# Normalising attention probabilities on GpSimd, with another written order of the first stage

## The chip, the cores and the metric

The kernel runs on one core of one Trainium2 chip. A core has five engines that run side by side, each with its own queue of instructions that it takes strictly in order: TensorE (PE in the profile, its weight loads PEld), VectorE (DVE), ScalarE (ACT), GpSimd (POOL) and SyncE (SP), which here only issues DMAs. The metric is device time in microseconds (us) for one execution.

## The reference

Three layers in a row, all in float32. The first is a windowed attention with block summaries:

```
k_sum = k.reshape(B, H, nb, 32, D).max(axis=3);  v_sum = v.reshape(...).mean(axis=3)
scores = concat[ scale*q@k.T where |i-j| < 16 else -1e9,  scale*q@k_sum + log(32) ]
a = exp(scores - max);   a = a / (sum(a) + 1e-9);   x = a @ concat[v, v_sum]
```

with 2 batches, 8 heads, 768 positions and head size 64. Its result, 1536 tokens of width 512, goes through `h = x @ w_in`, a PReLU with a slope for each of 2048 channels, and `@ w_out`. The last layer has four experts, `relu(x @ w1[e]) @ w2[e]`, summed with normalised weights. The attention inputs q and k are eight times as large as their first draw.

## The kernel before

**Precision.** A matmul operand is split into a high part (rounded by ScalarE) and a low part (the difference), and a product is three matmuls: high by high, high by low, low by high.

**First stage.** Attention and the first group of four of the sixteen 128-wide slices of the PReLU layer are done together. Attention is cut into 24 half tiles, numbered 0 to 23: 128 tokens by half of the heads. A 256-token block of the first group needs four half tiles (block 0 needs half tiles 0 to 3). The order of this stage is not left to a scheduler: `ORDER` (line 51) is a list of 695 short words, each one step, and every engine gets its instructions in the order of that list, inside `tc.manual_schedule()` (line 878). A word is a two-letter step and a number; a `g` or `v` behind the number moves the step to GpSimd or VectorE (line 880). The dictionary `stage` (line 864) says what a step is:

- `ka`, `va` load K and V by DMA, `kb`, `vb` reduce them over blocks on VectorE, `kc` copies the block maxima beside the keys; `vc` transposes the block sums on TensorE, `ve` (VectorE) and `vd` (ScalarE) write their two halves as means into the two value buffers.
- `fa`, `fb`, `fc` load keys, queries and values of a half tile.
- `sa` scores (TensorE), `sb` mask and row maximum (VectorE, line 225), `sc` exponential with row sums (ScalarE, line 234), `na` adds 1e-9 (VectorE, line 241), `nb` takes reciprocals (VectorE, line 244), `nc` multiplies the probabilities by them (`a_norm`, line 246), `ta` transposes (TensorE), `tb` copies the transposed block to SBUF (ScalarE), `xa` multiplies with the values (TensorE), `xb` and `xc` write high and low part of x (ScalarE, VectorE line 294).
- `wa` loads a slice ("piece") of `w_in` or `w_out` as raw 64-bit numbers; `wb` to `wj` turn it into float32 high and low parts: seven VectorE steps (`wb wd we wf wg wh wj`) and two on ScalarE (`wc`, `wi`). Pieces 0 to 3 are the first group's `w_in`, 4 to 7 its `w_out`, 8 to 15 the second group's.
- `la` multiplies (12 matmuls of 128x256), `lb` to `le` apply the PReLU and split; `ma` and `mb` are the product with `w_out` and the copy of its sum. `pa` is the first product of the second group.

`a_norm` has three forms:

```
if on != "a":
    eng = nc.vector if on == "v" else nc.gpsimd
    eng.tensor_tensor(pp, pp, r[:, :, None].to_broadcast([P, 4, NK]), op=ALU.mult)
    return
for u in range(4):
    nc.scalar.activation(pp[:, u], pp[:, u], AF.Copy, scale=r[:, u:u + 1])
```

The probability buffer `sm` exists three times, the PSUM buffer shared by `la`, `ta` and `vc` three times, the raw buffer of a piece three times.

**Later stages.** Behind the first stage come the other three groups of the PReLU layer and then the experts; their instructions are ordered by a scheduler when the program is built. GpSimd subtracts low parts there (line 387).

Of the kernel before, what the change touches and what calls it, by code (L numbers as in the profile page):

```python
# [48 lines left out]


ORDER = (
# [34 lines left out]
)  # L86
MASK_OFF = -1.0e9 * math.sqrt(D)
EXP_LOW = float((1023 - 127 + 20) << 20)
# [984 lines left out]
```

## Time and profile before

| what | value |
|---|---|
| time of 3 runs | median 838.79 us, 838.59 to 838.93 |
| the profiled execution | 837.95 us |
| its span, first to last instruction | 836.2 us |
| busy: PE, PEld | 814.4 us (97%), 745.3 us (89%) |
| busy: DVE, ACT, POOL | 618.2 us (74%), 427.4 us (51%), 294.0 us (35%) |
| chain that ended last, by engine | PE 92%, ACT 4%, DVE 2%, DMA 1% |

The profile follows one execution. Matmuls overlap each other, and the ends shown for them are modelled, so that a busy PE is not a PE at its peak. The chain is followed back from the last instruction, at each step to what released it or to the instruction before it on its engine. All but the first 152 us run after the first stage.

### The profile page before, as it was taken

Reading aid. Unit: us, or ns where it says so; the run is one execution under the profiler, and the core shown is the slowest. Engines: PE = TensorE matmul, PEld = TensorE weight load, DVE = VectorE, ACT = ScalarE, POOL = GpSimd, SP = SyncE. Lnnn points to the kernel's source line nnn. Section 1 sums busy time; section 2 is a strip of 40 time slices with the busy share of each in tenths; the row PEclk is TensorE's granted clock in tenths of the full one; section 3 lists DMA queues with packets and bytes.
Section 4 is the critical chain, followed back from the end, with each engine's and each line's share of the span. In section 5 each row is a group of like instructions: output and inputs, shape, how many; then the busy total and the mean of one; then the engine's idle time right before and its main releaser. Section 6 shows DMA issues by size and latency. Waiting matters only on the chain.

```text
span 836.2 us, 14453 instructions
## 1 busy us (share of the span) xinstructions
PE 814.4 (97%) x5000; PEld 745.3 (89%) x5000; DVE 618.2 (74%) x1315; ACT 427.4 (51%) x1050; POOL 294.0 (35%) x265
## 2 busy tenths in 40 slices
PE   3799999999999999999999999999999999999998
PEld 3699999888888888988988988988999999999997
DVE  6998667999994446587687687687667677768765
ACT  4999995543442323454454454455455454455430
POOL 0000000000013100376886886889243444354330
PEclk9799999999999999999999999999999999999999
DMA  9999412233222100266866867879776756767621
GB/s 321 283 299 298 156 46 102 101 100 102 84 92 74 53 1 0 101 223 229 304 234 231 290 215 252 289 240 321 241 228 203 256 197 229 238 217 231 200 74 75
DMA packets 97496, 155.37 MB, mean 186 GB/s; under 512 B 9872, under 2 KB 48272, under 8 KB 97424
## 3 DMA queue, kind: packets, MB, share of 16 engines
q1 hardware_dynamic: 96848, 154.18, 55.0%
q8 instruction: 39, 0.64, 0.3%
q14 instruction: 33, 0.27, 0.1%
q10 hardware_dynamic: 576, 0.28, 0.1%
HBM read 106.71 MB, written 47.71 MB: 185 GB/s over the span
## 4 chain that ended last, share of the span: by engine, by line
PE 92%; ACT 4%; DVE 2%; DMA 1%; issue 0%; ACTq 0%
PE l L536 48%; PE cb L655 16%; PE l2q L777 13%; PE cd L655 8%; PE ca L655 4%; PE s L215 1%; ACT sm L234 1%; ACT sm L253 1%; PE xps L277 1%; PE pt L259 1%; DMA alpha_sb<-in_alpha 1%; ACT ptb L152 1%; DMA kw<-in_kw 1%; DVE vs L179 0%; DVE sm L225 0%; DVE vcat L192 0%
## 5 line engine op out<-in xcount | busy, mean ns | idle before, releaser
L387 POOL TENSOR_TENSOR w0l<-ra,w0h 128x256 fp32r<-128x256 f32 (+1 forms) x32 | 36.8, 1151 | 357.4 <-ACT w0h L386 357.4
L824 DVE SCALAR_TENSOR_TENSOR acc<-l,prob_sb,acc 128x512 f32<-128x512 f32 x101 | 74.5, 745 | 24.7 <-PE l L536 24.6
L788 DVE SCALAR_TENSOR_TENSOR acc<-l2q,prob_sb,acc 128x256 f32<-128x256 f32 x156 | 71.2, 479 | 27.3 <-PE l2q L777 25.4
L536 PE MATMUL l<-xh,w0h 128*128 128x512 f32 (+1 forms) x240 | 84.6, 352 | 0.1
L536 PE MATMUL l<-gh,w1h 128*128 128x512 f32 (+1 forms) x240 | 83.4, 350 | 0.0
L536 PE MATMUL l<-xl,w0h 128*128 128x512 f32 (+1 forms) x240 | 83.3, 347 | 0.0
L536 PE MATMUL l<-xh,w0l 128*128 128x512 f32 (+1 forms) x240 | 83.2, 347 | 0.0
L536 PE MATMUL l<-gh,w1l 128*128 128x512 f32 (+1 forms) x240 | 83.0, 347 | 0.0
L536 PE MATMUL l<-gl,w1h 128*128 128x512 f32 (+1 forms) x240 | 81.5, 347 | 0.0
L536 PE MATMUL l<-w1h,gh 128*128 128x512 f32 x192 | 75.6, 394 | 0.0
L536 PE MATMUL l<-w1h,gl 128*128 128x512 f32 x192 | 75.2, 392 | 0.0
L536 PE MATMUL l<-w1l,gh 128*128 128x512 f32 x192 | 75.1, 391 | 0.0
L678 ACT ACTIVATE u<-cb 128x384 f32<-128x384 f32 x64 | 31.3, 489 | 51.7 <-PE cb L655 51.7
L561 DVE SCALAR_TENSOR_TENSOR l<-m,beta,l 128x512 f32<-128x512 f32 (+1 forms) x60 | 38.6, 646 | 23.8 <-ACT m L555 23.6
L555 ACT ACTIVATE m<-l 128x512 f32<-128x512 f32 (+1 forms) x60 | 30.6, 512 | 46.6 <-PE l L536 46.3
L536 PEld LDWEIGHTS l<-xh,w0h 128*128 128x128 f32 x240 | 45.5, 189 | 6.2 <-ACT ptb L152 0.3
L536 PEld LDWEIGHTS l<-gh,w1h 128*128 128x128 f32 x240 | 45.5, 189 | 5.7
L536 PEld LDWEIGHTS l<-gh,w1l 128*128 128x128 f32 x240 | 45.5, 189 | 5.6
L536 PEld LDWEIGHTS l<-xl,w0h 128*128 128x128 f32 x240 | 45.4, 189 | 5.5
L536 PEld LDWEIGHTS l<-gl,w1h 128*128 128x128 f32 x240 | 45.4, 189 | 5.5
L536 PEld LDWEIGHTS l<-xh,w0l 128*128 128x128 f32 x240 | 45.4, 189 | 5.6
L387 POOL TENSOR_TENSOR w0l<-s,w0h 128x512 fp32r<-128x512 f32 x32 | 47.8, 1513 | 2.9 <-ACT w0h L386 2.9
(165 smaller groups left out, 2527.7 us busy)
## 6 DMA issues: line engine op xcount, KB each, us to landing
raw<-in_wa SPq DMA_DIRECT2D x32, 512.0 KB, 3.8
rb<-in_wb SPq DMA_DIRECT2D x16, 512.0 KB, 4.5
ra<-in_wb SPq DMA_DIRECT2D x32, 256.0 KB, 3.6
dt<-xh SPq DMA_DIRECT2D x28, 256.0 KB, 3.4
dt<-xl SPq DMA_DIRECT2D x28, 256.0 KB, 4.3
bh<-dt SPq DMA_DIRECT2D x28, 256.0 KB, 3.7
bl<-dt SPq DMA_DIRECT2D x28, 256.0 KB, 3.6
q<-in_qh SPq DMA_DIRECT2D x24, 256.0 KB, 5.2
```

What stands on the lines that cost most here:

```text
L152: nc.scalar.activation(dst, src, AF.Copy)
L215: nc.tensor.matmul(sp[:, u], q[:, u // 2, u % 2], kw[:, :, u // 2, u % 2], start=True, stop=True)
L234: nc.scalar.activation(sm[:, u], sm[:, u], AF.Exp, bias=mx[:, u:u + 1], scale=-1.0, accum_out=sume[:, u:u + 1],)
L387: nc.gpsimd.tensor_tensor(lo, src, hi.bitcast(F32), op=ALU.subtract)
L536: ins = nc.tensor.matmul(ps, a, c, start=(i == 0), stop=(i == n - 1))
L555: nc.scalar.activation(m, gs[i, c0][0], AF.Relu, scale=-1.0)
L561: nc.vector.scalar_tensor_tensor(ps, m, beta[:, i:i + 1], ps, op0=ALU.mult, op1=ALU.add)
L655: nc.tensor.matmul(ps, l, r, start=(first and i == 0), stop=(i == len(terms) - 1), skip_group_check=True)
L678: nc.scalar.activation(v[name], ps, AF.Copy)
L777: nc.tensor.matmul(ps, l, r, start=(first and j == 0), stop=(j == len(terms) - 1), skip_group_check=True)
L788: nc.vector.scalar_tensor_tensor(dst, ps, pe, dst, op0=ALU.mult, op1=ALU.add)
L824: nc.vector.scalar_tensor_tensor(acc2[:, t], ps, pe, acc2[:, t], op0=ALU.mult, op1=ALU.add)
```

## The change

Only the text of `ORDER` is another. It holds the same 695 steps. 22 of the 24 `nc` steps (all but half tiles 2 and 16) carry a `g`: there one GpSimd `tensor_tensor` of 128x480 takes the place of four ScalarE activations of 128x120. All other steps stay on their engines, but nearly all stand at another place. What follows the first stage is the same on each engine, instruction by instruction. The table differs in all its lines; of it two:

```diff
@@ -49,40 +49,40 @@
 ORDER = (
-    "wa5 wd5 wb5 we5 ka01 wc5 kb01 ka00 fa2 kb00 kc00 fb2 sa2 wf5 wa3 wg5 fa0 wh5 wb3 wd3 fb0 wi5 ka03 "
...
+    "wa5 wb5 wc5 wa1 wd5 wa0 we5 wf5 ka01 ka00 ka03 wb1 wg5 wd1 fa4 fb2 wh5 wc1 wi5 wf1 wb0 fa2 ka02 "
...
```

On GpSimd the first rows after start-up were, in the kernel before (`w0l`, `s` and `ra` belong to the experts, `vs` to the block sums):

```order
7 L853 MEMSET vs 128x480
8 L387 ISA
9 L387 TENSOR_TENSOR w0l<-ra,w0h 128x256
10 L396 TENSOR_TENSOR s_3682<-ra 128x256
11 L397 TENSOR_TENSOR s_3682<-s_3682,ra 128x256
```

and are now (`sm` is the probabilities, `r` the reciprocals):

```order
7 L853 MEMSET vs 128x480
8 L250 ISA
9 L250 TENSOR_TENSOR sm<-sm,r 128x480 x22
10 L387 TENSOR_TENSOR w0l<-ra,w0h 128x256
11 L396 TENSOR_TENSOR s_3616<-ra 128x256
```

So the 22 multiplications stand ahead of all other work of GpSimd, on an engine that had none in this stage.

On ScalarE, about where the first batch's value means are written (`vcat`, line 190), there stood before (line 253 is the normalising, 234 the exponential, 152 a copy, 318 a step of a piece):

```order
25 L190 ACTIVATE vcat_102<-vsps 24x512
26 L190 ACTIVATE vcat_103<-vsps 24x512
27 L253 ACTIVATE sm<-sm,r 128x120 x4
28 L152 ACTIVATE ptb<-pt 120x512
29 L234 ACTIVATE sm,sume<-sm,mx 128x120 x4
30 L152 ACTIVATE w0h<-t 128x512
```

and now:

```order
21 L190 ACTIVATE vcat_102<-vsps 24x512
22 L190 ACTIVATE vcat_103<-vsps 24x512
23 L234 ACTIVATE sm,sume<-sm,mx 128x120 x4
24 L318 ACTIVATE e<-e,ebias 128x512
25 L152 ACTIVATE xh<-xps 128x2x128
26 L152 ACTIVATE ptb<-pt 120x512
```

The exponential of half tile 7 now stands directly behind the two `vcat` writes.

On VectorE, after its own half of the `vcat` writes (line 192), there stood before:

```order
99 L192 TENSOR_SCALAR vcat_102<-vsps 24x512
100 L192 TENSOR_SCALAR vcat_103<-vsps 24x512
101 L241 TENSOR_SCALAR r<-sume 128x4
102 L338 SCALAR_TENSOR_TENSOR e<-raw,e 128x512
103 L244 RECIPROCAL r<-r 128x4
104 L330 SCALAR_TENSOR_TENSOR t<-raw,t 128x512
```

and now, there and at the reciprocals of half tiles 5 (row 134) and 6 (row 139):

```order
103 L192 TENSOR_SCALAR vcat_102<-vsps 24x512
104 L192 TENSOR_SCALAR vcat_103<-vsps 24x512
105 L323 TENSOR_SCALAR t<-raw 128x512
106 L356 TENSOR_TENSOR w0l<-t,w0h 128x512
107 L241 TENSOR_SCALAR r<-sume 128x4
...
134 L244 RECIPROCAL r<-r 128x4
135 L334 TENSOR_SCALAR e<-e 128x512
136 L330 SCALAR_TENSOR_TENSOR t<-raw,t 128x512
137 L241 TENSOR_SCALAR r<-sume 128x4
138 L338 SCALAR_TENSOR_TENSOR e<-raw,e 128x512
139 L244 RECIPROCAL r<-r 128x4
```

Row 107 reads the row sums of half tile 7; before, row 101 read those of half tile 6, whose exponential stood ahead of the `vcat` writes.

## Rows read from the trace of the kernel before

**Rows 1.** Busy time by stretch; its first line names the columns.

```profile
core 0: us, PE busy (x) PEld busy (x) DVE busy (x) ACT busy (x) POOL busy (x), PEclk, DMA share, GB/s
0.00:40.00 40.00, 22.09 (x124) 18.91 (x124) 32.90 (x125) 28.33 (x99) 0.73 (x6) 0.88 0.91 302
40.00:72.00 32.00, 31.67 (x364) 29.31 (x364) 31.27 (x130) 31.80 (x121) 0.00 (x0) 0.99 0.92 288
72.00:152.00 80.00, 79.73 (x786) 77.46 (x785) 58.49 (x199) 65.49 (x226) 0.00 (x0) 1.00 0.41 135
```

**Rows 2.** The chain up to 340 us: start us, us, what ran.

```profile
65.46 1.51 ACT sm L234 x8
...
67.51 1.69 PE l L536 x12
69.19 0.88 PE s L215 x8
70.08 0.61 PE xps L277 x16
...
75.20 0.44 PE pt L259 x4
75.64 2.87 PE l L536 x24
...
129.82 206.64 PE l L536 x984
```

**Rows 3.** Timeline of DVE and PE: start us, us, engine, line, what.

```profile
43.96 0.42 DVE L294 TENSOR_TENSOR xl<-xps,xh 128x256 fp32r<-128x256 f32 x1
44.88 0.36 PE L536 MATMUL l<-xh,w0h 128*128 128x256 f32 x1
...
68.55 0.75 DVE L294 TENSOR_TENSOR xl<-xps,xh 128x256 fp32r<-128x256 f32 x2
69.21 1.34 DVE L356 TENSOR_TENSOR w1l<-t,w1h 128x512 fp32r<-128x512 f32 x2
70.62 0.39 PE L536 MATMUL l<-gh,w1h 128*128 128x256 f32 x1
```

**Rows 4.** The chain from 18 to 34 us, where DVE carries it.

```profile
19.09 0.60 DVE w1l L356
...
22.60 0.20 DVE sm L225
```

**Rows 5.** Waits of DVE up to 70.6 us: total, times, longest.

```profile
DVE t L323 <- DMA raw<-in_wa: 4.8, 1, 4.8
DVE r L241 <- ACT sm L234: 0.9, 2, 0.7
DVE ksum L169 <- DMA acc<-in_kt: 0.7, 1, 0.7
```

**Rows 6.** Timeline of the normalising and of the value means.

```profile
16.18 1.24 ACT L253 ACTIVATE sm<-sm,r 128x120 f32<-128x120 f32 x4
...
30.99 1.31 DVE L192 TENSOR_SCALAR vcat<-vsps 24x512 f32<-24x512 f32 x2
32.39 1.07 ACT L190 ACTIVATE vcat<-vsps 24x512 f32<-24x512 f32 x2 [0.80 <-DVE vcat L192]
```

**Rows 7.** Timeline of POOL from 347 us.

```profile
348.08 2.54 POOL L387 TENSOR_TENSOR w0l<-s,w0h 128x512 fp32r<-128x512 f32 x2
350.60 0.73 POOL L387 TENSOR_TENSOR w0l<-ra,w0h 128x256 fp32r<-128x256 f32 x1
```

**Rows 8.** Timeline of POOL and DVE from 361 us.

```profile
361.03 3.44 POOL L387 TENSOR_TENSOR w0l<-s,w0h 128x512 fp32r<-128x512 f32 x2
361.55 0.74 DVE L822 TENSOR_SCALAR acc<-l,prob_sb 128x512 f32<-128x512 f32 x1
```

**Rows 9.** Two lines of DVE: ns min/median/max, first and last start.

```profile
L330 DVE SCALAR_TENSOR_TENSOR t<-raw,t x32: 660/686/701, 5.5 to 246.4; 128x512 f32<-128x512 uint32 x32
L437 DVE TENSOR_TENSOR rb<-rb x28: 1110/1458/1818, 359.8 to 553.1; 128x512 f32<-128x512 f32 x28
```

66 rows, old and new, of the table ORDER are left out of this document.

## Prediction

> **What bounds the kernel now.** I read busy time by stretch first [rows 1]. The first stage ends near 152 us; whatever follows it has the same instructions in the same order before and after, so the change moves the end by as much as it moves the moment at which TensorE (PE) leaves this stage. From 40 to 72 us PE is busy 31.67 of 32 us, from 72 to 152 us 79.73 of 80. Only the first 40 us have room: 22.09 us busy, at a mean granted clock of 0.88. From 40 to 72 us three engines are full at once: VectorE (DVE) 31.27, ScalarE (ACT) 31.80, PE 31.67. After 72 us DVE needs 58.49 of 80 us.
>
> The chain came second [rows 2]. It runs on ACT up to about 67 us and from there on PE without a break; the row that starts at 129.82 is one piece of 206.64 us. So what comes late ahead of 72 us is paid in full, and what is freed later is worth nothing.
>
> Third, the two places at which PE takes over the results of the others [rows 3]. The first product of the first group (`la`) starts at 44.88, behind the low half of x that DVE starts at 43.96. The first product with `w_out` (`ma`) starts at 70.62; it needs piece 4, whose low half is the second of the two instructions that end at 69.21 + 1.34 = 70.55. Between the two PE issues 8 `la` (2.87 / 2 = 1.435 us each), 7 `sa` (0.88), 5 `ta` (0.44) and 7 `xa` (0.61) [rows 2]: 11.5 + 6.2 + 2.2 + 4.3 = 24.1 us in 25.7, so PE lost 1.6 us there. Behind 70.62 it hardly waits. That is the gate to work out: when does DVE deliver piece 4, and what has PE done by then.
>
> **The change part by part.**
>
> ScalarE. One normalising is four activations, 1.24 us [rows 6]; 22 x 1.24 = 27.3 us leave ACT, 11 of them (13.6 us) ahead of the first `ma`. As PE was full beside it, no more than the 1.6 us that PE lost can come back there, and a little at the first `la`.
>
> GpSimd (POOL). 512 columns took 2.54 / 2 = 1.27 us, 256 took 0.73 [rows 7]; for 480 an estimate between them is 0.73 + (224 / 256) x 0.54 = 1.20 us. 22 of them are 26 us on an engine that was idle for the whole stage [rows 1]. For the half tile itself 1.20 stands for 1.24: no gain and no loss.
>
> DVE's queue. I counted the steps ahead of piece 4's low half in both orders. Before there are 15 `sb`, 8 `wj` and 10 `xc`, now 14, 7 and 9; every other DVE step has the same number. An `sb` is four times 0.20 us and a `wj` 0.60 [rows 4], an `xc` (69.21 - 68.55) / 2 = 0.33 [rows 3]: 1.73 us less. With waits as before, piece 4 would be there at 70.55 - 1.73 = 68.82. PE has one `sa` less to do ahead of its first `ma` (16 for 17), the rest is equal: 0.88 us. So the end stays the same if `ma` starts at 70.62 - 0.88 = 69.74. With 0.07 us from DVE's end to PE's start, as now, DVE has 69.74 - 0.07 - 68.82 = 0.85 us to give away.
>
> DVE's waits. Up to 70.6 us it waited 4.8 us for the first piece, which stays, then 0.9 for row sums from ACT and 0.7 for a load of K [rows 5]. The K loads now stand behind two more pieces in SyncE's queue, but DVE has some twenty steps of pieces 5, 1 and 0 ahead of them; I let the 0.7 go and the 0.9 stay. The first scores come some 7 us later by that (an estimate), which PE can afford, since DVE's queue is what it waits for. New is a wait at the value means: ACT's two writes began at 32.39, right at the end of DVE's two (30.99 + 1.31) although ACT had been idle for 0.80 us [rows 6]. Behind ACT's writes now stands the exponential of half tile 7, 1.51 us [rows 2], and DVE, with only a mask and a low half (0.34 as an estimate, and 0.60) to do meanwhile, comes to its row sums: 0.1 + 1.07 + 1.51 - 0.94 = 1.7 us of wait, and everything behind it in DVE's queue moves, the x of the first block too. Net +1.0; the bounds are -1.6 (all waits go, none comes) and +1.7.
>
> DVE against POOL. Late in the kernel, where both work, an instruction of DVE with two SBUF inputs and 512 columns took 1.458 us (L437, median), while one of that size took 0.686 with POOL idle (L330) [rows 9]; POOL's own took 3.44 / 2 = 1.72 for 1.27 [rows 7, 8]. In between, one that reads PSUM and writes SBUF took 0.74 [rows 8]. So the two hold each other up where a two-input step of a piece (`we wg wh wj`) meets a multiplication. Ahead of the first `ma` 11 multiplications run; the bounds are 0 and 11 x 1.20 = 13.2 us. I went through what stands on DVE within 1.2 us behind each reciprocal. For half tiles 1, 0, 7, 9, 10 and 11 it is reductions, masked maxima and steps out of PSUM: nothing. For 3, 4 and 8 the next two-input step is either running already, so that POOL waits, or far off. Behind the reciprocal of 5 two such steps follow at once: about 1.05 us. Behind that of 6 come the masked maxima (0.80) and then one: 0.55. I take 1.6 us, near the lower end, as the written order puts few of them together.
>
> Sum: 68.82 + 1.0 + 1.6 + 0.07 = 71.49 for the first `ma`, against 69.74: **1.75 us later**. Behind it the other 11 multiplications can cost DVE 13.2 us at most, of 80 - 58.49 = 21.5 us that it has free [rows 1]; PE keeps what it has. The profiled execution took 837.95 us, a span of 836.2 and 1.75 around it; it becomes 839.7. The median of the runs is 0.84 above the profiled one: 840.5. Contention of 1.0 to 2.6 and net waits of 0 to 1.7 give this case 838.9 to 842.2.
>
> **The rivals.**
>
> *DVE's one-input steps wait as well.* `wb`, `wd` and `wf` read one SBUF tile and write another. No row of before shows one of them beside a POOL instruction. If they are held up too, three more places count: half tile 3 (1.2 us), 4 (1.1) and 8 (0.75), less 0.3 that falls into other waits: +2.75, so 4.5 us later, 843.3. For it speaks that the two-input ones do wait, against it that the PSUM one did not. The Trainium skill, SBUF — State Buffer, section "Who interferes with whom", counts copies and `tensor_scalar` from SBUF to SBUF among those that take the ports shared with GpSimd and hold them for the whole instruction; by that rule this rival holds and the sum is 843.3, by the PSUM row alone it does not.
>
> *ACT was the limit, and the kernel gets faster.* The chain lies on ACT up to 67 us [rows 2], ACT was full [rows 1], and 13.6 us of its work ahead of the first `ma` go. If the multiplications fall into gaps and DVE waits for nothing behind its start, piece 4 is there at 68.82 - 1.6 = 67.2, 2.4 us under the mark, and PE gets back the 1.6 us that it lost and 0.8 at the first `la`: 2.4 us faster, 836.4. It decides as soon as piece 4 comes ahead of 69.67. Against it: DVE was as full as ACT (31.27 of 32) and waited for ACT only 0.9 us [rows 5], so that a lighter ACT has little to give it.
>
> *PE's own queue decides.* DVE loses no more than the 0.85 us that it may, and PE is full as before: no change, 838.8. For it: PE stood at 31.67 of 32 us. Against it: the wait at the value means alone is more.
>
> **How the numbers follow.** The forecast gets 0.40, the one-input rival 0.22, PE's queue 0.20, faster through ACT 0.18. About 0.2%, 1.7 us, is what a measurement of this kernel can tell from no change. Slower by more: half of the forecast's case, all of the first rival and a little of the third, 0.44. Faster by more: 0.16, most of the ACT case. Within: 0.40. Predicted is 840.5 us; the range of 836.8 to 843.4 leaves out the outer part of the ACT case and what lies past the first rival; the likeliest case alone spans 838.9 to 842.2.
>
> **What would show it.** In the profile after: POOL with 22 instructions of about 1.2 us between 25 and 130 us; ACT idle in places between 40 and 72 us; DVE waiting for ACT's exponential behind its `vcat` writes for some 1.7 us; two-input steps of DVE of over 1.2 us beside POOL, at half tiles 5 and 6; the first `la` near 45 and the first `ma` near 71.5 us; PE without idle time behind it. Steps of 0.42 us that last over 1 us would speak for the first rival. The forecast is wrong if the first `ma` starts ahead of 69.7 us, or if PE idles behind 72 us.

## The result and the profile after

| | before | after |
|---|---|---|
| time, median of 7 runs each | 838.59 us (837.70 to 840.52) | 842.97 us (841.02 to 845.48) |
| ratio, 95% interval | 1 | 1.0061 (1.0047 to 1.0076) |
| span of the profiled execution | 836.2 us | 840.6 us |
| first `la`, first `ma` start | 44.88, 70.62 us | 46.19, 72.40 us |
| PE starts on the next stage | 151.31 us | 155.73 us |

The kernel became 4.4 us slower, and all of it is made in the first stage: 155.73 - 151.31 = 4.42 us at its end, 840.6 - 836.2 = 4.4 us over the span. From there to the end the twelve profiles of this document, those of the experiments included, all take 684.7 to 685.4 us.

Busy time by stretch after the change; the columns are those of [rows 1], the third stretch is 4 us longer.

```profile
0.00:40.00 40.00, 17.89 (x107) 15.88 (x108) 31.64 (x109) 19.96 (x67) 5.24 (x10) 0.87 0.87 286
40.00:72.00 32.00, 31.60 (x359) 29.67 (x358) 31.97 (x131) 27.40 (x99) 6.91 (x7) 0.95 0.98 293
72.00:156.00 84.00, 82.21 (x808) 79.83 (x808) 65.21 (x213) 56.41 (x192) 11.33 (x11) 1.00 0.42 133
```

ScalarE got its relief: 27.40 us where it had 31.80 [rows 1]. VectorE is now full without a gap (31.97 of 32). PE does 4.2 us less in the first 40 us, and behind 72 us it leaves 1.8 of 84 us unused, where it left 0.27 of 80.

The timeline of DVE and PE at the two places of [rows 3]: start us, us, engine, line, what.

```profile
44.98 0.75 DVE L294 TENSOR_TENSOR xl<-xps,xh 128x256 fp32r<-128x256 f32 x2
45.58 0.69 PE L277 MATMUL xps<-ptb,vcat 120*64 120x64 f32 x16
46.19 0.39 PE L536 MATMUL l<-xh,w0h 128*128 128x256 f32 x1
...
70.90 0.68 DVE L356 TENSOR_TENSOR w1l<-t,w1h 128x512 fp32r<-128x512 f32 x1
72.03 0.61 PE L215 MATMUL s<-kw,q 128*128 128x120 f32 x4
72.40 0.36 PE L536 MATMUL l<-gh,w1h 128*128 128x256 f32 x1
```

At the first `la` PE comes 0.46 us behind DVE's x, with other work in between. At the first `ma` it is different: piece 4 ends at 70.90 + 0.68 = 71.58, and PE starts on it 0.82 us later, straight out of scores. Before, that gap was 0.07 us [rows 3]. So piece 4 does not decide; PE is late by itself. Nor did it decide before: there PE went from its products with the values straight on to the first `ma`, with nothing but PE in the chain of waits ([rows 2], 70.08 and 70.69), and that piece 4 had ended 0.07 us earlier was chance.

PE's busy time from the first `la` to the first `ma` (stretch, us, busy, granted clock, DMA share, GB/s):

```profile
46.19:72.40 26.21, 25.81 (x292) 1.00 1.02 302
```

and the row with which it comes out of its wait for the value means, ahead of the first `la`:

```profile
37.44 1.97 PE L277 MATMUL xps<-ptb,vcat 120*64 120x64 f32 x32 [2.75 <-ACT vcat L190]
```

Between the two places PE idles 0.40 us in all, and from 37.44 us to the first `la` it works without a gap as well, at a granted clock of 0.55 and 0.60 in the two stretches of 4 us from 36 to 44 us.

What DVE waited for up to 80 us (total, times, longest), to compare with [rows 5]:

```profile
DVE e L310 <- DMA raw<-in_wa: 5.5, 1, 5.5
DVE r L241 <- ACT sm L234: 1.8, 1, 1.8
DVE beta L856 <- DMA alpha_sb<-in_alpha: 1.0, 1, 1.0
```

The wait for row sums behind the value means is the 1.8; two at the very start were not foreseen: the first piece lands 0.7 us later (5.5 for 4.8), and `alpha` comes late. Of the 0.7 us most belongs to this execution: in the five kernels below that begin with the same steps and loads (order_only, sc7, loads, spread, act34) the first piece is there at 4.90 to 5.03. The wait for `alpha` is 0.9 to 1.0 us in all of them.

DVE beside GpSimd's multiplications (L250), at half tiles 3, 4 and 5:

```profile
25.20 1.27 POOL L250 TENSOR_TENSOR sm<-sm,r 128x480 f32<-128x480 f32 x1 [23.94 <-DVE r L244]
25.55 1.21 DVE L334 TENSOR_SCALAR e<-e 128x512 uint32<-128x512 f32 x1
26.68 0.94 DVE L179 TENSOR_REDUCE vs<-acc 128x24 f32<-128x768 f32 x1
...
32.61 0.65 DVE L344 TENSOR_TENSOR t<-t,e 128x512 f32<-128x512 f32 x1
32.86 1.25 POOL L250 TENSOR_TENSOR sm<-sm,r 128x480 f32<-128x480 f32 x1 [1.94 <-ACT sm L234]
33.19 0.95 DVE L241 TENSOR_SCALAR r<-sume 128x4 f32<-128x4 f32 x1
...
45.98 0.99 POOL L250 TENSOR_TENSOR sm<-sm,r 128x480 f32<-128x480 f32 x1 [2.22 <-ACT sm L234]
46.03 1.48 DVE L330 SCALAR_TENSOR_TENSOR t<-raw,t 128x512 f32<-128x512 uint32 x1
```

Read the ends. POOL's first multiplication ends at 26.47, the one-input step that began beside it at 26.76, which is 0.29 us after POOL's end: it stood until POOL was through. The tiny 128x4 step at 33.19 (0.17 us elsewhere) ends 0.03 us behind POOL's 34.11. POOL is held up in turn: with a two-input step of DVE still running in front of it, it takes 1.25 to 1.27 us, alone 0.99.

Last, a stretch of the chain of waits behind 72 us, where PE before was busy 79.73 of 80 us [rows 1]: start us, us, what.

```profile
88.68 4.48 DMA q<-in_qh
93.15 0.14 issue
93.29 1.14 PE s L215 x8
...
94.82 0.43 SPq L197
95.25 0.05 issue
95.30 4.37 DMA kw<-in_kw
99.67 0.14 issue
99.80 1.12 PE s L215 x8
```

Twice PE stands before scores whose queries or keys are still under way (0.91 and 0.80 us idle in the timeline). SyncE's queue tells why; its waits from 70 to 101 us begin with this row:

```profile
SPq L202 <- PE s L215: 15.0, 5, 5.3
```

A load of q (L202) waits for TensorE to finish scores, since `q` has three buffers. In the new order `fb21` stands far ahead (issued near 60 us), but `sa21` comes last, after `sa20`, `sa18` and `sa22` (near 105 us), and `fb22` is issued ahead of `fb20` and `fb18`. So 21 holds one of the three buffers all that time and 22 a second one from 88 us on; 20 and 18 must go through the third, one behind the other: `sa20` at 93.29 releases the load of 18 at 94.44.

### The profile page after: what moved, and what is told of

The parts are those of the page before. It is cut to its first block, busy times and chain, and to the rows that moved or that the text cites. A ratio compares the mean times of both kernels' runs of the same rounds, so it can differ in the third digit from the quotient of the medians.

```text
span 840.6 us, 14439 instructions
## 1 busy us (share of the span) xinstructions
PE 813.1 (97%) x5000; PEld 745.2 (89%) x5000; DVE 623.2 (74%) x1315; ACT 404.9 (48%) x962; POOL 318.9 (38%) x287
## 4 chain that ended last, share of the span: by engine, by line
PE 91%; DVE 6%; DMA 2%; issue 0%; ACT 0%; POOL 0%; ACTq 0%; SPq 0%
PE l L536 48%; PE cb L655 16%; PE l2q L777 12%; PE cd L655 8%; PE ca L655 4%; PE s L215 1%; DVE sm L225 1%; DMA alpha_sb<-in_alpha 1%; PE xps L277 1%; DVE ksum L169 1%; PE pt L259 1%; DMA q<-in_qh 1%; DVE t L330 1%; DMA kw<-in_kw 1%; DVE t L344 0%; DVE e L338 0%
## 5 line engine op out<-in xcount | busy, mean ns | idle before, releaser
L387 POOL TENSOR_TENSOR w0l<-ra,w0h 128x256 fp32r<-128x256 f32 (+1 forms) x32 | 38.6, 1205 | 238.0 <-ACT w0h L386 238.0
L250 POOL TENSOR_TENSOR sm<-sm,r 128x480 f32<-128x480 f32 x22 | 22.7, 1035 | 100.6 <-DVE r L244 52.4
```

The costliest lines, as they stand in the source:

```text
L387: nc.gpsimd.tensor_tensor(lo, src, hi.bitcast(F32), op=ALU.subtract)
```

## The experiments

All numbers in one table; each time is the median of its runs, the ratio is to the kernel before on the same chip (837.91, 837.96 or 838.49 us in the three sets). Starts in us from the profile.

| kernel | time | ratio (95%) | first `la` | first `ma` | next stage |
|---|---|---|---|---|---|
| after (above) | 842.97 | 1.0061 (47 to 76) | 46.19 | 72.40 | 155.73 |
| order_only | 852.56 | 1.0172 (156 to 187) | 47.93 | 78.71 | 165.91 |
| pool_only | 839.48 | 1.0016 (06 to 26) | 43.73 | 70.04 | 150.89 |
| sc7 | 841.75 | 1.0046 (28 to 64) | 45.26 | 71.63 | 154.52 |
| loads | 840.61 | 1.0027 (17 to 38) | 45.30 | 73.56 | 155.36 |
| alpha | 841.67 | 1.0041 (27 to 55) | 44.56 | 71.81 | 154.88 |
| spread | 841.17 | 1.0041 (27 to 56) | 45.59 | 73.86 | 157.12 |
| act34 | 841.88 | 1.0043 (28 to 57) | 44.88 | 72.94 | 156.25 |
| mended | 838.86 | 1.0014 (02 to 25) | 43.27 | 70.13 | 151.26 |
| all | 836.93 | 0.9996 (-22 to 14) | 43.41 | 69.14 | 150.28 |
| pick | 838.04 | 1.0001 (-15 to 17) | 43.63 | 69.16 | 149.59 |

(The bounds are the last four digits: 47 to 76 is 1.0047 to 1.0076.) The profiled executions of `loads` and `spread` were the slowest of their kernels' runs, by 1.3 and 2.6 us over the median, and that of `act34` was 1.5 us over it: their starts are those of a late run, and the ratio decides there. Those of pool_only and pick were the fastest of theirs, by 1.2 and 1.5 us.

In four profiles the first `la` comes 0.6 to 1.6 us earlier than after the change (0.5 to 0.7 of that is the first piece, which is there earlier) and the first `ma` does not follow: it is 1.2, 1.5 and 0.5 us later in loads, spread and act34, and 0.6 earlier in alpha. PE waits in between, in loads for row sums (2.0 us), in the others for loads of values and, in spread, for ScalarE as well. The row of alpha, then that of act34:

```profile
PE xps L277 <- DMA vcat<-in_vw: 1.3, 2, 1.0
PE xps L277 <- DMA vcat<-in_vw: 1.8, 2, 1.1
```

### The order alone, and GpSimd alone

order_only is the new list without its `g`; pool_only the old list with the 22 `g`.

```diff
 order_only:  - nc3g nc1g nc4g ... nc23g      + nc3 nc1 nc4 ... nc23
 pool_only, in the old list:  - nc0 nc4 nc1 ... + nc0g nc4g nc1g ...
```

Expected of order_only: 

> The new written order alone, all 24 multiplications on ScalarE. Theory A (several small waits ahead of the first la, of which steps of DVE held up beside GpSimd are about 1.8 us, and ScalarE needs the relief in this order): the held-up steps return to their own 0.34 to 0.6 us, but between 40 and 72 us ScalarE gets 7 x 1.24 = 8.7 us to the 27.4 it has, 36.1 of 32, and becomes late by some 4 us: first la near 46, first ma near 75, end 2 to 3 us later than the changed kernel, 844 to 846. Rival B (GpSimd is the whole cause, the order is harmless): first ma near 70, end as before, 838.5 to 839.5.

Expected of pool_only: 

> The old written order, with the same 22 multiplications on GpSimd. Theory A (GpSimd holds DVE up only where a step from SBUF to SBUF lies beside it, and the old order puts some there by chance): DVE loses 1 to 3 us ahead of the first ma, ScalarE's relief gives back at most 1.6: end 0 to 2 us later than before, 838.6 to 840.6. Rival B (GpSimd is the whole cause): about 843, as the changed kernel. Rival C (ScalarE was the limit in the old order): 836.4.

The order without GpSimd costs 14.65 us, twice what was expected; without GpSimd's share it is far worse than with it. ScalarE has 30.70 of 32 us in the stretch in which it had 27.40, short of the 36 that were expected to overfill it, but it is late, and others wait for it (busy time, then waits of DVE up to 72 and of PE up to 160 us):

```profile
40.00:72.00 32.00, 29.47 (x281) 26.34 (x281) 25.88 (x111) 30.70 (x111) 0.00 (x0) 0.82 0.77 231
```

```profile
DVE r L241 <- ACT sm L234: 6.0, 6, 1.8
...
PE pt L259 <- ACT sm L253: 4.2, 5, 1.5
```

GpSimd without the order costs 1.57 us. Its trace shows a gain and a loss. The wait of DVE for row sums from ACT [rows 5] and that for K are gone, and the first `la` starts 1.2 us earlier than before. But three steps ahead of it are held up by GpSimd:

```profile
25.66 1.48 DVE L344 TENSOR_TENSOR t<-t,e 128x512 f32<-128x512 f32 x1
...
36.80 1.14 DVE L356 TENSOR_TENSOR w0l<-t,w0h 128x512 fp32r<-128x512 f32 x1
38.20 1.14 DVE L330 SCALAR_TENSOR_TENSOR t<-raw,t 128x512 f32<-128x512 uint32 x1
```

Each takes 0.65 to 0.69 otherwise. So rival B, that GpSimd is the whole cause, falls in both runs; the two parts do not add up either, since the new order needs the relief. The profile of pool_only reaches the next stage 0.4 us earlier than before, while its runs are 1.57 us slower: one profile, here of the fastest run, does not settle differences of that size.

### The wait behind the value means

```diff
- sb7 nb0 ve0 vd0 wa6 sc7
+ sb7 sc7 nb0 ve0 vd0 wa6
```

> The changed kernel with the exponential of half tile 7 written ahead of the value means on ScalarE. Theory A: DVE's wait of 1.8 us for row sums behind the value means goes, the means themselves come some 0.2 us later: first la 1.5 us earlier (44.7), end 1.5 us earlier, 841.4. Rival: PE's first product with the values, which waited 2.8 us for the means, now comes later by the exponential (1.5 us) and takes the place of the wait: first la not before 46, 843.

DVE's wait for row sums at half tile 7 is gone from the trace. Others take part of its place: DVE waits 0.6 us for a buffer that a transpose frees and 0.6 that the profile puts down to POOL, and PE's wait for the means stays, with a new one (waits of DVE up to 72, of PE up to 160 us):

```profile
DVE sm L225 <- PE pt L259: 0.6, 1, 0.6
DVE sm L225 <- POOL sm L250: 0.6, 1, 0.6
```

```profile
PE xps L277 <- ACT vcat L190: 2.7, 1, 2.7
PE s L215 <- DVE r L244: 1.8, 1, 1.8
```

The first `la` comes 0.93 us earlier, of which 0.5 is the first piece's load in this execution. By the ratio the gain is 0.15% (1.2 us), within the intervals. Theory A has the wait right, which went; that its going is worth anything is not shown by this run alone, and 1.2 us is less than the 1.8 that it lasted.

### The loads of q

```diff
- nc11g fb21 we4 ... xa15 fb22 le20 ... ta14 fb20 wa8
- sa20 fb18 fa22 fa18 ... na19 sa18 wg10
+ nc11g we4 ... xa15 fb20 le20 ... ta14 fb18 fa18 wa8
+ sa20 fb22 fa22 ... na19 sa18 fb21 wg10
```

> The changed kernel with the loads of q for half tiles 21 and 22 issued after those of 20 and 18, so that they don't hold two of the three q buffers until 100 us, and K of 18 ahead of K of 22. Theory A: the two waits of PE for q and kw at 93 and 100 us (0.9 and 0.8) go; first la and first ma stay at 46.2 and 72.4, the stage ends 1.7 us earlier (154.0), 841.3. Rival (another engine is as late there, the DMA only came last): the waits turn into waits for DVE or ScalarE, 843.

Behind 76 us PE waits for no load any more; this is all that is left there:

```profile
PE vsps L184 <- ACT ptb L152: 0.4, 1, 0.4
```

The ratio falls from 1.0061 to 1.0027, the only single edit whose interval lies apart from that of the changed kernel: 0.34%, 2.9 us, more than the 1.7 expected, with an uncertainty of about half of it. The first `la` and `ma` were expected to stay; in the profile, a late run, they moved, and the next stage is reached only 0.4 us earlier. The runs of sc7 and spread, which kept the old loads, wait there still (1.5 us for kw in each).

### Alpha

```diff
+    nc.scalar.dma_start(out=alpha_sb, in_=alpha)
     nc.scalar.dma_start(out=mask, in_=mask_in)
     nc.scalar.dma_start(out=ident, in_=ident_in)
     ...
-    nc.scalar.dma_start(out=alpha_sb, in_=alpha)
```

> The changed kernel with only the load of alpha moved to the front of ScalarE's queue, ahead of mask and ident. Theory A (the wait for alpha is a term of its own): DVE's wait of 1.0 us at beta goes and what follows keeps 0.5 to 1.0 of it: first la near 45.3, end 0.5 to 1 us earlier, 842. Rival (alpha lands earlier, but the second and third piece land as late as before, and DVE waits for these instead): no change, 843.

DVE's start now is one wait, with the first piece at its end (its step starts at 4.8 for 5.5):

```profile
DVE beta L856 <- DMA alpha_sb<-in_alpha: 4.7, 1, 4.7
```

The first `la` is 1.6 us earlier (0.7 of it the first piece), the next stage 0.85; by the ratio 0.20%, 1.7 us, within the intervals. The rival falls by these waits, in which no later piece takes alpha's place; that the time gains is not clear of the noise.

### Steps held up by GpSimd, in two ways

```diff
 spread
- nb3 wj0 wf2 va03 nc3g ta3 sa0 vb00 wg2 ... sa5 na0 fa6 fc2 wb3 wi2 nc4g sb7 nb0
+ nb3 va03 nc3g ta3 sa0 vb00 wj0 wf2 wg2 ... sa5 fa6 fc2 wi2 nc4g sb7 na0 wb3 nb0
 act34
- nc3g ... nc4g
+ nc3 ... nc4
```

> The changed kernel, all 22 multiplications on GpSimd, with five DVE steps in another order: behind the reciprocal of half tile 3 now comes a sum of V (0.86) and then wj and wf, behind that of half tile 4 the masked maxima of 7 (0.80) and then na and wb. Theory A (DVE and GpSimd shut each other out whenever a DVE step goes from SBUF to SBUF by the fast path, of one input too; sums and steps out of PSUM run beside it): wf and na fall from 1.21 and 0.95 us to 0.42 and 0.17, first la some 1.4 us earlier (44.8), end 1.4 earlier, 841.5. Rival (one-input steps are not held up by GpSimd, their length came from elsewhere): steps stay long, 843.

> The changed kernel with the multiplications of half tiles 3 and 4 back on ScalarE (eight activations, 2.5 us), the other 20 on GpSimd. Theory A (these two held DVE up by 0.8 us each, and ScalarE, busy 20 of the first 40 us, has room for them): wf and na fall to 0.42 and 0.17 us, first la 1.0 to 1.6 us earlier, end as in the run with the five DVE steps moved, 841 to 842. Rival (ScalarE's queue, which the new order plans without them, passes the delay on to the exponentials and value means): first la as late as 46 us or later, 843 to 845.

In spread the same steps, with the same multiplications near them, now start when POOL is through, or at its very end (timeline of DVE and POOL):

```profile
24.49 0.92 DVE L179 TENSOR_REDUCE vs<-acc 128x24 f32<-128x768 f32 x1
24.72 0.99 POOL L250 TENSOR_TENSOR sm<-sm,r 128x480 f32<-128x480 f32 x1 [23.46 <-DVE r L244]
25.33 0.93 DVE L356 TENSOR_TENSOR w0l<-t,w0h 128x512 fp32r<-128x512 f32 x1
26.18 0.41 DVE L334 TENSOR_SCALAR e<-e 128x512 uint32<-128x512 f32 x1
...
32.33 1.25 POOL L250 TENSOR_TENSOR sm<-sm,r 128x480 f32<-128x480 f32 x1 [2.31 <-ACT sm L234]
33.46 0.17 DVE L241 TENSOR_SCALAR r<-sume 128x4 f32<-128x4 f32 x1
```

L334 falls from 1.21 to 0.41 us, L241 from 0.95 to 0.17; the sum of V (one input, a reduction) runs beside POOL in 0.92, as without it. In act34 the same two steps take 0.43 and 0.16 us with the multiplications on ACT. The rival of spread is refuted by these rows, that of act34 by its first `la` of 44.88. Both kernels gain 0.18 to 0.20% by the ratio, 1.5 to 1.7 us, which is what was expected of the held-up steps but lies within the intervals; so the hold-up is shown, its price is not. In spread's profile the first `la` was to come 1.4 us earlier and comes 0.6.

### All of it, and a choice for the old order

mended is sc7, loads and alpha together, with one more word moved (`ta4` ahead of `xa3 xa2`, which wait for the value means); all is mended and spread; pick is the old order with `g` on 0, 4, 5, 7, 9 and 12 to 23 save 16.

```diff
 mended
- fa8 xa3 xa2 fb8 wc3 wd3 fc4 ta4 ta0
+ fa8 ta4 xa3 xa2 fb8 wc3 wd3 fc4 ta0
 pick, in the old order
- nc0 nc4 nc5 nc7 nc9
+ nc0g nc4g nc5g nc7g nc9g
```

> The changed kernel with the exponential of 7 ahead of the value means, the transposes of half tile 4 ahead of the products of 3 and 2 with the values, alpha loaded first on ScalarE's queue, and the q and kw loads in the order of the run with the loads. Theory A (the loss is a sum of waits of the written order: 1.8 row sums, 0.9 alpha, 1.7 late loads): DVE's offset at half tile 7 falls by 2.7, PE waits for no load behind 90 us, end 3 to 4.4 us earlier, 838.6 to 840. Rival (each wait hides another of the same size): 841 to 842.

> The last kernel with the five DVE steps moved away from GpSimd's multiplications as well. Theory A (contention adds to the waits): 1.4 us less than that kernel, 837.2 to 838.6, so as before or a little faster. Rival (waits and contention overlap): as that kernel.

> The old written order with GpSimd for the multiplications of half tiles 0, 4, 5, 7, 9 and all from 12 on, beside which no DVE step ahead of the first ma was held up in the run of the old order with all 22; the others back on ScalarE. Theory A (contention took back what ScalarE's relief gave there): DVE's offset at piece 4 is about 7 to 8 us for 9.4, first ma near 69, end 1 to 2 us earlier than before: 836 to 837.5. Rival (ScalarE is full again): as before, 838.

mended gives back 0.47% of the 0.61%, 3.9 us, without touching what GpSimd does, and its interval lies apart from that of the changed kernel; all gives another 0.18%, with intervals that overlap mended's. The first products of all (timeline of PE):

```profile
42.80 0.69 PE L277 MATMUL xps<-ptb,vcat 120*64 120x64 f32 x16 [0.46 <-ACT sm L234]
43.41 0.39 PE L536 MATMUL l<-xh,w0h 128*128 128x256 f32 x1
...
69.14 0.36 PE L536 MATMUL l<-gh,w1h 128*128 128x256 f32 x1
```

First `la` 2.8 us earlier than after the change, first `ma` 3.3, and PE waits for nothing between 76 and 152 us. The first `la` is no earlier than mended's 43.27: DVE has both low halves of x ready there by 41.94, and PE comes late, with waits that the profile puts down to loads of queries and values (0.94 and 0.90 us, up to 37.52 and 39.57). The single edits come to 0.34 + 0.20 + 0.15 = 0.69% for loads, alpha and sc7, against 0.47 measured together: they may hide each other in part, but intervals of this width allow a plain sum too. The median of all, 836.93, is 1.03 us under that of before, but its interval reaches from -0.22 to +0.14%: no slower, and not shown to be faster. pick shows no gain either (1.0001), as its rival had it, though its one profile, of the fastest run, reached the next stage 1.7 us earlier.

## Why the prediction was right and wrong

The direction was right; of the 4.4 us it gave 1.75.

**DVE's sum held, by luck.** Forecast for the end of piece 4 was 71.42 us; measured are 71.58. Waits and contention together were to move DVE by 1.0 + 1.6 = 2.6 us; the times of its steps taken off, it runs 2.8 us later than before at that point. The wait behind the value means is 1.79 (1.7). Contention at half tile 5 is 0.8 us (1.05), at 6 0.3 to 0.4 (0.55). Left out were the later start (0.65), alpha (0.9) and the one-input steps (half tiles 3 and 4, 0.8 each, 8 0.4), 3.5 us in all. Against these 6.5 us stand some 3.7 of waits and small gaps of the old order behind its first piece (6.5 - 2.8, an estimate): all of them went, where the forecast let only the 0.7 of the K load go. The sum came out by two errors that cancel.

**The first step that failed is the gate.** The forecast put it at the first `ma`, because piece 4 ended there 0.07 us ahead of PE; but PE came without waiting, before and after, and piece 4 was ready in time by chance before and 0.82 us ahead of PE after. PE's own account shows where the time is lost. PE has one `sa` (0.88) and one `ta` (0.44) less to do ahead of the first `la`, so it had to start at 44.88 - 1.32 = 43.56 for the end to stay, and starts at 46.19: 2.63 us late. From there to the first `ma` PE loses 1.7 us, as it lost 1.6 before, and arrives 72.40 - 69.74 = 2.66 us late, past DVE, which could have let it in 0.75 us earlier. What DVE loses between the two places can cost no more than the 0.40 us that PE idles there. What it loses ahead of the first `la` (the start 0.65, alpha 0.9, half tiles 3 and 4 1.6, the value means 1.8) is what can move it; how much each of these cost is not shown, as the runs that take one of them away lie within the intervals. mended and all move the first `la` to 43.27 and 43.41; of the loss 0.14% is left by mended's ratio (interval 0.02 to 0.25) and nothing by that of all.

**"PE keeps what it has" failed as well, and by more**: 1.7 us more are lost behind 72 us, in two waits for loads, the sign by which the forecast said that it would be wrong. The forecast put this term at nothing because DVE has free time there, and did not look at SyncE's queue; loads takes these waits away, and with 0.34% it is the one single edit clear of the noise. 2.66 + 1.76 = 4.42 is the measured whole. In the forecast's terms, of the 4.42 - 1.75 = 2.67 us that it missed, 1.76 are lost behind the first `ma`, 0.75 are PE's lateness behind piece 4, and 0.16 DVE's sum.

**A reading of the chain.** Before, it does not stay on PE from 67 us on: between 86.50 and 93.08 us it runs over the value means, exponentials and normalisings of the second batch, on DVE and ACT. PE idled little all the same (0.27 us from 72 to 152), so that the sum does not hang on it; but what feeds PE there had no time to spare.

**The rivals.** The first, that one-input steps wait as well, came to 843.3, next to the measured 842.97, with the right mechanism and by luck in its size: one-input steps were held up by 2.0 us in all, 1.6 of it ahead of the first `la`, not by 2.75, and the loads of q, which it does not have, cost 1.7. The Trainium skill, SBUF — State Buffer, section "Who interferes with whom", has steps with two SBUF inputs, and `tensor_scalar` where it runs in a mode that takes both of VectorE's ports, shut out for the whole of a GpSimd instruction that came first, and reductions never; the rows agree: 1.48 for 0.68 us with two inputs, 1.21 for 0.41 and 0.95 for 0.17 (128x4) with one, and 0.92 for a sum beside POOL. The second rival, ACT as the limit, falls: in the old order, with the same relief, the first `la` comes 1.2 us earlier, yet the time rises by 0.16% (pool_only). The third needed DVE to lose no more than 0.85 us; it lost 2.8.

**Smaller terms.** A multiplication takes 0.99 us on GpSimd, not 1.20: the estimate came from a line that writes fp32r and reads unbroadcast operands; which of the two makes the difference is not shown. ScalarE's relief was taken as worth little; order_only shows that without it this order costs 10 us more, so it is a condition of the order rather than a gain.

**Open.** How the 2.63 us at the first `la` divide among the start, alpha, the held-up steps and the value means; how much of the difference between mended and all is contention and how much the clock (below); whether all is truly faster than before, for which 12 runs do not do.

## What to carry to other kernels

Look for the place from which the engine that bounds the end hardly waits any more, and price the change there; that another engine's result is ready just as it comes there does not make it wait. An earlier arrival at that place helps only as far as what it needs next is ready too (alpha, act34). When a written order moves, follow the queue of loads with its buffers as closely as the compute engines: a load issued early that is used late takes a buffer from all those between. Work given to GpSimd held VectorE up here wherever VectorE at that moment went from SBUF to SBUF, and not where it reduced or read PSUM; a few moved words freed the steps as well as taking the work back did (spread, act34).

## What was not expected of the hardware

TensorE's granted clock fell to 0.50, 1.2 of 2.4 GHz, in most profiles of this stage, at places that differ. Two rows of the changed kernel (busy time of PE in stretches of 4 us, granted clock, DMA share, GB/s), then one of all by the stretch up to 40 us with all engines:

```profile
28.00:32.00 4.00, 3.86 (x17) 0.50 0.97 370
...
40.00:44.00 4.00, 4.00 (x47) 0.60 0.83 235
```

```profile
0.00:40.00 40.00, 16.43 (x134) 14.02 (x136) 34.41 (x133) 23.82 (x80) 5.94 (x11) 1.00 0.90 299
```

In the changed kernel PE had been idle up to 17.2 us, then busy 3.72 of 4 us from 20 on at full clock, before it fell; in all it was idle up to 15.8, and the clock stayed at 1.00 throughout. mended fell as deep (0.87 over the first 40 us) and still had its first `la` at 43.27, and the kernel before had 0.50 from 32 to 40 us, so a low clock by itself does not make the first `la` late. In the changed kernel it lasted until 44 us: eight `sa` matmuls take 1.83 us from start to next start at 41.10 and 0.98 at 44.60. But DVE, which waited for nothing of PE's up to there, ends x only at 45.73, and the first matmul that reads this low half, the second of the `la`, starts at 46.42: a full clock could have brought it forward by 0.7 us at most. It may be a part of what runs of one kernel differ by (841.02 to 845.48 for the changed one); no run here tells that apart.

A reduction (0.92 us) or a step out of PSUM (the value means, 1.31 us for the two as before) ran beside GpSimd at its usual length, while a step of 128x4 was held up by 0.78 us, as long as one of 128x512 (0.80): what counted was the moment, not the size.
